# Tail rows of ten heads' query weights loaded by two DMAs of eight rows each

## The chip, the cores and the metric

One core of a Trainium2 chip runs the whole program. The metric is the device time of one execution in microseconds, the median of several runs. Inputs and outputs lie in the chip's main memory (HBM); the core works on data in SBUF, a memory of 128 partitions, and 16 DMA engines bring the data in.

## The reference

Two layers with the same weights and caches, on two rows of 448 numbers, all in float32. A layer is attention against a given cache (16 heads of 256, 4096 cached positions per row and head), then a gated feed-forward block. The core of it:

```python
def _A_ref(x, k_cache, v_cache, wq, wo):          # B=2, Sq=1, D=448, H=16, Sk=4096, Dh=256
    q = (x @ wq).reshape(B, Sq, H, Dh).transpose(0, 2, 1, 3)
    scores = jnp.einsum("bhqd,bhkd->bhqk", q, k_cache) * (Dh ** -0.5)
    p = _softmax(scores, axis=-1)
    o = jnp.einsum("bhqk,bhkd->bhqd", p, v_cache)
    return o.transpose(0, 2, 1, 3).reshape(B, Sq, H * Dh) @ wo
def _B_ref(x, W_gate, W_up, W_down):              # 448 -> 1792 -> 448
    gate = jnp.einsum("bsd,df->bsf", x, W_gate)
    up = jnp.einsum("bsd,df->bsf", x, W_up)
    return jnp.einsum("bsf,fd->bsd", gate * (gate > 0) * up, W_down)
x = A_x
x = x + _A_ref(_layernorm(x), ...)
x = x + _B_ref(_layernorm(x), ...)
x = x + _A_ref(_layernorm(x), ...)   # the second layer
x = x + _B_ref(_layernorm(x), ...)
```

## The kernel before

The two caches are 268 MB together and are needed in both layers, so nearly all of the program's traffic is the reading of K and V. A unit of work is one head and one of the two rows of x: 32 units per layer, in the order of `first`, and in the second layer backwards (`second`). The K and the V of a unit are one block of 4096 KB each, which lands as 32 KB on each of the 128 partitions. SBUF holds an arena of 27 places of 8 KB per partition: six blocks of four places, and three single places. Heads' weights always go to a single place. At the end of the first layer 22 places are kept for the second.

The loads stand in a list, `pending`, which is put together when the program is built. `pump` takes the next entry when a place is free, and writes a DMA into the queue of SyncE (SP). All of these loads stand in SP's one queue and go out in that order. An issue waits until the last reader of the place that it overwrites is done (TensorE, as a rule), and for the transfer that last used its semaphore; eight semaphores (DMAHW0 to DMAHW7 in the rows of order below) are used in turn. `release` frees a place after its last matmul and calls `pump` again. At the beginning and end of a layer blocks are split into pieces of 1024 KB or 512 KB.

The weights of a head are one load, `w_head[name]`: 1792 numbers on each of the 128 partitions. They hold, for the 448 rows of that head's query weights, three full chunks of 128 rows (3 x 256 numbers), then the remaining 64 rows (the tail), then the two chunks of the head's output weights (2 x 448). The tail is folded: the left half of its 256 columns lies on partitions 0 to 63, the right half on partitions 64 to 127, 128 numbers each.

`query` computes the query of a head for both rows of x: for each half of the 256 columns, three matmuls over the full chunks (line 309) and one over the tail (line 312). The tail's matmul takes all 128 partitions; `xT[:, FULL + j, :]` is zero on the half that doesn't belong to column half j, since `mask` is zero there. VectorE then copies the result to `q_pad` (line 317). `score` multiplies the query with a K block (line 333), `weigh` the probabilities with a V block (line 393), `project` multiplies with the output weights. `ffn` streams the feed-forward weights in seven loads `in` and four loads `out` (line 512 and line 249).

Of the kernel before, what the change touches and what calls it, by code (L numbers as in the profile page):

```python
# [14 lines left out]
B, D, H, S, DH, F = 2, 448, 16, 4096, 256, 1792  # L15
P = 128
DC = 5
FULL, TAIL = 3, 64
NT = S // P
CT = 8  # L20
UNIT = CT * DH
NC = NT // CT
BLOCKS, SINGLES = 6, 3
KEPT = 22

G, E = 4, 4
# [39 lines left out]
def two_layers(  # L66
# [3 lines left out]
    k_cache: bass.AP,  # L70
    v_cache: bass.AP,
    w_head: bass.AP,
    w_in: bass.AP,
    w_out: bass.AP,
    out: bass.AP,
):
    nc = tc.nc
# [10 lines left out]
    arena = consts.tile([P, (BLOCKS * NC + SINGLES) * UNIT], F32, name="arena")  # L88
# [8 lines left out]
    def source(key, n):  # L97
        kind, name, c = key
        if kind in "kv":
            h, b = name  # L100
            if kind == "k":
                rows = k_cache[b, h]
            else:
                rows = v_cache[b, h].rearrange("(p t) d -> p (t d)", t=NT)
            return rows[:, c * UNIT : (c + n) * UNIT]
        if kind == "h":
            return w_head[name]
        if kind == "in":
            return w_in[c]
        return w_out[:, (14 * c + 2) // 4 * D : (14 * c + 16) // 4 * D]  # L110

    def pump():
        while pending:
            at = None
            for i, ((kind, name, c), n) in enumerate(pending[: AHEAD if pending[0][1] == 1 else 1]):
                if i and kind != "h":
                    continue
                last = at_of.get((kind, name, c - 1)) if kind in "kv" else None
                at = units.take(n, kind, last)
                if at is not None:  # L120
                    break
            if at is None:
                return
            pending.pop(i)
            src = source((kind, name, c), n)
            dst = arena[:, at * UNIT : at * UNIT + src.shape[1]]
            parts = [0, src.shape[1]]
            if kind == "v" and n == 1 and c == NC - 1 and name in (first[-1], second[-1]):
                parts[1:1] = [UNIT // 2]
            if not pending:  # L130
                parts[1:1] = [src.shape[1] - D]
            for i, j in zip(parts, parts[1:]):
                nc.sync.dma_start(dst[:, i:j], src[:, i:j])
            for k in range(n):
                at_of[kind, name, c + k] = at + k

    def get(*key):
        at = at_of[key]
        return arena[:, at * UNIT : (at + 1) * UNIT]

    def release(*key):
        units.free.add(at_of.pop(key))
        pump()
# [31 lines left out]

    keep = {of_second[0], *[key for key in of_second if key[0] != "h"][:KEPT]}
    of_second = [key for key in of_second if key not in keep]
# [40 lines left out]
    xT = xr[:, :, :, 0]  # L218
# [48 lines left out]
    def again():  # L267

        for half in range(2):
            n = D - DH if half else DH  # L270
            nc.tensor.matmul(
                y[32 * half : 32 * half + B, :n], halves[:, half], yrow[:, :n],
                start=True, stop=False,
            )
# [16 lines left out]
    def attention(order, after):  # L291
# [8 lines left out]
        def query(u):  # L300
            h = order[u][0]
            w = get("h", h, 0)
            pq = pq_all
            for j in range(2):
                if j and u == 0:
                    again()
                for c in range(FULL):
                    at = c * DH + j * P
                    nc.tensor.matmul(  # L309
                        pq[:, j, :], w[:, at : at + P], xT[:, c, :], start=(c == 0), stop=False  # L310
                    )
                nc.tensor.matmul(  # L312
                    pq[:, j, :], w[:, FULL * DH : FULL * DH + P], xT[:, FULL + j, :],
                    start=False, stop=True,
                )
            q = q_pad[:, u // 2 % 2]
            nc.vector.tensor_copy(q[..., 1], pq)
            for v in (u, u + 1):
                q_of[v] = q[:, :, order[v][1]]
# [23 lines left out]
        def score_turn(u):  # L343
            s_of[u] = ps_s.tile([P, NT], F32, name="small")
            s = s_of[u].rearrange("p (h e g) -> p h e g", h=2, e=E)
            for e in range(E):
                nc.tensor.matmul(  # L347
                    s[:, :, e, :], found_s[:, e * P : (e + 1) * P], pick,
                    start=True, stop=True,
                )  # L350
# [7 lines left out]
        def softmax_exp(u):  # L358
            b = order[u][1]
            nm = work.tile([P, 1], F32, name="nm")  # L360
            nc.scalar.activation(nm, mx_of.pop(u), AF.Copy, scale=nsr[:, b : b + 1])  # L361
            p_of[u] = work.tile([P, NT], F32, name="probs")
            rs = work.tile([P, 1], F32, name="rs")
# [64 lines left out]
        def project(u):  # L428
            h = order[u][0]
            if u % 2 == 0:  # L430
                return
            wo = get("h", h, 0)[:, FULL * DH + P :]
            for c in range(2):
                add(
                    c, oT_of[h][:, c, :], wo[:, c * D : (c + 1) * D],
                    start=(c == 1 and u == 1), stop=(u == n_u - 1),
                )
            if ("h", h, 0) not in after:
                release("h", h, 0)
            if u == n_u - 1:  # L440
                busy(1, 0)
# [54 lines left out]
        busy(1, 0)  # L496
        out_keep(u)
        project(u)

    def ffn(last):  # L500
# [104 lines left out]
def _arrays(np, A_x, A_k_cache, A_v_cache, A_wq, A_wo, B_W_gate, B_W_up, B_W_down, **_):  # L605

    rows = FULL * P
    wq = A_wq.reshape(D, H, DH)
    head = [wq[c * P : (c + 1) * P].transpose(1, 0, 2) for c in range(FULL)]
    head.append(wq[rows:].reshape(TAIL, H, 2, P).transpose(1, 2, 0, 3).reshape(H, P, P))  # L610
    wo = A_wo.reshape(H, 2, P, D)
    head += [wo[:, 0], wo[:, 1]]
    full = [w[c * P : (c + 1) * P] for w in (B_W_gate, B_W_up) for c in range(FULL)]
    full.insert(FULL, np.concatenate([B_W_gate[rows:], B_W_up[rows:]]))
    down = B_W_down.reshape(4, D, D)
    chunks = [down[j, m * P : (m + 1) * P] for j in range(4) for m in range(FULL)]
    chunks += [np.concatenate([down[j, rows:], down[j + 1, rows:]]) for j in (0, 2)]
    k = A_k_cache.reshape(B, H, P, 2, E, G, 2, P).transpose(0, 1, 7, 3, 6, 5, 4, 2)
    found = {
        "x": A_x,  # L620
        "k_cache": k.reshape(B, H, P, S * 2),
        "v_cache": A_v_cache,
        "w_head": np.concatenate(head, axis=2),
        "w_in": np.stack(full),
        "w_out": np.concatenate(chunks, axis=1),
    }
    return {n: np.ascontiguousarray(a) for n, a in found.items()}
# [24 lines left out]
```

## Time and profile before

| | |
|---|---|
| time, median of 3 runs | 1325.39 us (1325.19 to 1327.15) |
| the profiled execution | 1327.24 us, of which the span is 1325.1 us |
| TensorE matmul busy | 938.0 us, 71% of the span |
| VectorE, ScalarE, GpSimd busy | 135.2, 92.1 and 47.7 us |
| DMA traffic | 561.53 MB in the main queue, 99.3% of 16 engines' time |

The span is the time from the first to the last instruction of the core that the profiler recorded; the rest of the execution lies outside it. The DMA share is the mean busy share of the 16 DMA engines: at 0.50, eight of them are busy, or all of them half the time. "The chain that ended last" follows the program back from its end, from each piece of work to what released it.

### The profile page before, as it was taken

The numbers are of one execution on the slowest core, as the hardware profiler recorded it, in microseconds if no ns is written. First come the engines' busy times: TensorE is split into PE (matmuls) and PEld (weight loads), VectorE is DVE, ScalarE is ACT, GpSimd is POOL, SyncE is SP. The second block draws the span as 40 slices with busy tenths as digits, with TensorE's granted clock in tenths as the row PEclk, the third lists the DMA queues.
The fourth block names the chain that finished last, engine by engine and source line by source line (L and its number), as shares of the span: only waits on it lengthen the run. The fifth ranks groups of instructions, "written<-read, shape, count | busy, mean of one in ns | idle before, by whom it ended". The sixth has DMA issues, their size and how long they took to land.

```text
span 1325.1 us, 13766 instructions
## 1 busy us (share of the span) xinstructions
PE 938.0 (71%) x6066; PEld 308.3 (23%) x6066; DVE 135.2 (10%) x457; ACT 92.1 (7%) x280; POOL 47.7 (4%) x134
## 2 busy tenths in 40 slices
PE   4867667767776776567688867766676676766668
PEld 2322122222221221222233322222122221222213
DVE  1101010011000110001101111010010100101100
ACT  1000000000000000000011100000000000000001
POOL 0000000000000000000000000000000000000000
PEclk9777787687667776877898897777777778778779
DMA  9999999999999999999999999999999999999997
GB/s 404 429 432 428 433 427 433 429 432 427 430 431 433 427 434 426 433 432 429 420 379 395 438 426 433 428 432 429 432 429 431 430 430 430 427 435 427 435 420 323
DMA packets 28151, 562.40 MB, mean 424 GB/s; under 512 B 3126, under 2 KB 3260, under 8 KB 10556
## 3 DMA queue, kind: packets, MB, share of 16 engines
q1 hardware_dynamic: 28084, 561.53, 99.3%
q8 instruction: 47, 0.77, 0.2%
q14 instruction: 12, 0.10, 0.0%
q10 hardware_dynamic: 8, 0.01, 0.0%
HBM read 561.52 MB, written 0.00 MB: 424 GB/s over the span
## 4 chain that ended last, share of the span: by engine, by line
PE 59%; another core or an unknown queue 21%; DMA 11%; DVE 3%; issue 1%; ACT 1%; POOL 0%; SPq 0%; POOLq 0%; ACTq 0%
PE rawa L333 12%; PE poa L393 12%; PE rawb L333 11%; PE pob L393 11%; DMA arena<-in_v_cache_dram 7%; PE small L347 4%; PE small L417 3%; PE pq L309 3%; DVE found_s L341 3%; DMA arena<-in_w_in_dram 2%; DMA arena<-in_w_out_dram 2%; PE pq L312 1%; PE y L249 1%; ACT probs L364 1%
## 5 line engine op out<-in xcount | busy, mean ns | idle before, releaser
L333 PE MATMUL rawa<-arena,q_pad 128*2 128x512 f32 x1024 | 186.0, 863 | 113.3 <-DMA arena<-in_k_cache_dram 112.8
L333 PE MATMUL rawb<-arena,q_pad 128*2 128x512 f32 x1024 | 177.4, 829 | 100.1 <-DMA arena<-in_k_cache_dram 100.1
L393 PE MATMUL poa<-arena,probs 128*2 128x512 f32 x1024 | 168.9, 821 | 62.3 <-DMA arena<-in_v_cache_dram 33.9
L393 PE MATMUL pob<-arena,probs 128*2 128x512 f32 x960 | 163.1, 841 | 47.4 <-DMA arena<-in_v_cache_dram 46.9
L347 PE MATMUL small<-ident,found_s 128*128 128x8 f32 x512 | 68.6, 260 | 35.6 <-DVE found_s L341 35.2
L347 PEld LDWEIGHTS small<-ident,found_s 128*128 128x128 f32 x512 | 62.8, 193 | 96.5 <-DVE found_s L341 96.5
L333 PEld LDWEIGHTS rawa<-arena,q_pad 128*2 128x2 f32 x1024 | 25.0, 96 | 210.9 <-issue 209.7
L393 PEld LDWEIGHTS poa<-arena,probs 128*2 128x2 f32 x1024 | 31.5, 105 | 171.6 <-issue 117.3
L361 ACT ACTIVATE nm<-top,nsr 128x1 f32<-128x1 f32 x64 | 18.8, 294 | 740.7 <-POOL top L356 740.7
L333 PEld LDWEIGHTS rawb<-arena,q_pad 128*2 128x2 f32 x1024 | 24.1, 96 | 198.3 <-DMA arena<-in_k_cache_dram 124.5
L356 POOL PARTITION_ALL_REDUCE top<-mx x64 | 22.5, 351 | 1166.1 <-DVE mx L354 1148.8
L417 PEld LDWEIGHTS small<-ones,row 128*128 128x128 f32 x256 | 43.3, 240 | 90.4 <-issue 83.9
L393 PEld LDWEIGHTS pob<-arena,probs 128*2 128x2 f32 x960 | 27.8, 105 | 156.9 <-issue 156.5
L309 PE MATMUL pq<-xs,arena 128*128 128x2 f32 x384 | 56.4, 263 | 0.0
L309 PEld LDWEIGHTS pq<-xs,arena 128*128 128x128 f32 x384 | 52.7, 208 | 2.6 <-issue 1.3
L426 DVE COPY oT<-small 128x2 f32<-128x2 f32 x64 | 10.2, 160 | 382.2 <-PE small L417 382.2
L417 PE MATMUL small<-ones,row 128*128 128x1 f32 x256 | 48.7, 294 | 0.4 <-ACT row L404 0.4
L409 DVE SCALAR_TENSOR_TENSOR row<-pob,ri,row 128x256 f32<-128x256 f32 x30 | 14.5, 484 | 205.3 <-ACT row L404 205.3
L409 DVE SCALAR_TENSOR_TENSOR row<-poa,ri,row 128x256 f32<-128x256 f32 x32 | 15.5, 484 | 170.4 <-ACT row L404 170.4
L404 ACT ACTIVATE row<-pob,ri 128x256 f32<-128x256 f32 x32 | 15.2, 474 | 231.9 <-PE pob L393 223.6
L341 DVE COPY found_s<-rawb 128x512 f32<-128x512 f32 x32 | 22.1, 692 | 88.0 <-PE rawb L333 88.0
L341 DVE COPY found_s<-rawa 128x512 f32<-128x512 f32 x32 | 22.1, 692 | 74.1 <-PE rawa L333 74.1
(81 smaller groups left out, 307.9 us busy)
## 6 DMA issues: line engine op xcount, KB each, us to landing
arena<-in_k_cache_dram SPq DMA_DIRECT2D x59, 4096.0 KB, 54.5
arena<-in_v_cache_dram SPq DMA_DIRECT2D x58, 4096.0 KB, 55.2
arena<-in_w_head_dram SPq DMA_DIRECT2D x31, 896.0 KB, 54.9
arena<-in_w_in_dram SPq DMA_DIRECT2D x14, 896.0 KB, 16.4
arena<-in_v_cache_dram SPq DMA_DIRECT2D x12, 1024.0 KB, 12.3
arena<-in_k_cache_dram SPq DMA_DIRECT2D x8, 1024.0 KB, 13.8
arena<-in_w_out_dram SPq DMA_DIRECT2D x4, 896.0 KB, 16.8
arena<-in_v_cache_dram SPq DMA_DIRECT2D x4, 512.0 KB, 47.5
```

The lines of the kernel that those rows point to most:

```text
L249: nc.tensor.matmul(bank[at : at + B, : w_h.shape[1]], stat, w_h, **flags)
L309: nc.tensor.matmul(pq[:, j, :], w[:, at : at + P], xT[:, c, :], start=(c == 0), stop=False)
L312: nc.tensor.matmul(pq[:, j, :], w[:, FULL * DH : FULL * DH + P], xT[:, FULL + j, :], start=False, stop=True,)
L333: nc.tensor.matmul(raw[u % 2][32 * g : 32 * g + 2, :], q_of[u][:, j, 1 - half : 3 - half], kt[:, g, :], start=(c == 0), stop=(c == NC - 1),)
L341: nc.vector.tensor_copy(found_s, raw[u % 2])
L347: nc.tensor.matmul(s[:, :, e, :], found_s[:, e * P : (e + 1) * P], pick, start=True, stop=True,)
L356: nc.gpsimd.partition_all_reduce(mx_of[u], mx, P, RED.max)
L361: nc.scalar.activation(nm, mx_of.pop(u), AF.Copy, scale=nsr[:, b : b + 1])
L393: nc.tensor.matmul(po_of[u][32 * t : 32 * t + 2, :], p_of[u][:, n : n + 2], vt[:, 2 * t * DH : (2 * t + 2) * DH], start=(c == 0), stop=(c ...
L404: nc.scalar.activation(row[:, :DH], po_of[u][:, :DH], AF.Copy, scale=r_of[u][:, 0:1])
L409: nc.vector.scalar_tensor_tensor(row[:, :DH], po_of.pop(u)[:, DH:], r_of[u][:, 1:2], row[:, :DH], op0=ALU.mult, op1=ALU.add,)
L417: nc.tensor.matmul(pT_of[u][:, c : c + 1], row[:, c * P : (c + 1) * P], ones, start=True, stop=True,)
```

## The change

For heads 2 to 11 the 64 tail rows leave the head's one load. The load is then 1664 numbers per partition. The tail comes as two further DMAs in front of it, each of 8 rows of 4 KB; a row holds four weight rows of 256 numbers, which go to four neighbouring partitions. The first DMA fills partitions 0 to 31, the second partitions 32 to 63. In HBM the rows are 4352 bytes apart (64 unused numbers follow each), so that a row doesn't continue the one before. The other six heads keep the folded form, whose tail now stands at the end of their load. The bytes read per head are the same.

```diff
+APART = range(2, 12)
+HEAD = FULL * DH + 2 * D
...
         if kind == "h":
-            return w_head[name]
+            return w_head[name, :, : HEAD if name in APART else HEAD + P]
...
             dst = arena[:, at * UNIT : at * UNIT + src.shape[1]]
+            if kind == "h" and name in APART:
+                for i in range(2):
+                    nc.sync.dma_start(
+                        arena[32 * i : 32 * i + 32, at * UNIT + HEAD : at * UNIT + HEAD + DH],
+                        w_tail[name, i, :, : 4 * DH].rearrange("e (r n) -> e r n", n=DH),
+                    )
...
-                nc.tensor.matmul(
-                    pq[:, j, :], w[:, FULL * DH : FULL * DH + P], xT[:, FULL + j, :],
-                    start=False, stop=True,
-                )
+                if h in APART:
+                    at = HEAD + j * P
+                    nc.tensor.matmul(
+                        pq[:, j, :], w[:TAIL, at : at + P], xT[:TAIL, FULL, :],
+                        start=False, stop=True,
+                    )
+                else:
+                    nc.tensor.matmul(
+                        pq[:, j, :], w[:, HEAD : HEAD + P], xT[:, FULL + j, :],
+                        start=False, stop=True,
+                    )
...
-            wo = get("h", h, 0)[:, FULL * DH + P :]
+            wo = get("h", h, 0)[:, FULL * DH : HEAD]
...
-    head.append(wq[rows:].reshape(TAIL, H, 2, P).transpose(1, 2, 0, 3).reshape(H, P, P))
+    tail = np.zeros((H, 2, 8, 4 * DH + 64), A_wq.dtype)
+    tail[..., : 4 * DH] = wq[rows:].transpose(1, 0, 2).reshape(H, 2, 8, 4 * DH)
     wo = A_wo.reshape(H, 2, P, D)
     head += [wo[:, 0], wo[:, 1]]
+    head.append(wq[rows:].reshape(TAIL, H, 2, P).transpose(1, 2, 0, 3).reshape(H, P, P))
```

SP's queue early in the first layer, before: one head's load, the four blocks that follow, and the next head's load. Sizes are partitions x numbers; in brackets stands what an issue waits for.

```order
L133 DMA arena<-in_w_head_dram 128x1792 [waits PE_49]
L133 DMA arena<-in_v_cache_dram 128x8192 [waits DMAHW0_49,PE_49]
L133 DMA arena<-in_k_cache_dram 128x8192 [waits DMAHW1_49,PE_49]
L133 DMA arena<-in_v_cache_dram 128x8192 [waits DMAHW3_49,DMAHW2_49,PE_49]
L133 DMA arena<-in_k_cache_dram 128x8192 [waits DMAHW4_49,PE_49]
L133 DMA arena<-in_w_head_dram 128x1792 [waits PE_49]
```

The same place in the program after: the block in front of a head, the head's three transfers, and the four blocks behind.

```order
L142 DMA arena<-in_k_cache_dram 128x8192 [waits DMAHW0_49,PE_49]
L132 DMA arena<-in_w_tail_dram 32x1x256 [waits DMAHW1_49]
L132 DMA arena<-in_w_tail_dram 32x1x256 [waits DMAHW2_49]
L142 DMA arena<-in_w_head_dram 128x1664 [waits DMAHW3_49,PE_49]
L142 DMA arena<-in_v_cache_dram 128x8192 [waits DMAHW4_49,PE_49]
L142 DMA arena<-in_k_cache_dram 128x8192 [waits DMAHW5_49,PE_49]
L142 DMA arena<-in_v_cache_dram 128x8192 [waits DMAHW6_49,PE_49]
L142 DMA arena<-in_k_cache_dram 128x8192 [waits DMAHW7_49,PE_49]
```

Two tail transfers now stand ahead of a head's load, so there are seven issues instead of five for every four blocks, and the turn of the eight semaphores comes round sooner.

TensorE, the query of one head in the first layer, before, with the first V product behind it:

```order
L309 MATMUL pq<-xs,arena 128x2 [waits DMAHW2_49]
L309 MATMUL pq<-xs,arena 128x2 x2
L312 MATMUL pq<-xs,arena 128x2
L309 MATMUL pq<-xs,arena 128x2 x3
L312 MATMUL pq<-xs,arena 128x2
L393 MATMUL pob<-arena,probs 2x512 [waits DMAHW3_49,Activation_49]
```

The same after:

```order
L318 MATMUL pq<-xs,arena 128x2 [waits DMAHW4_49]
L318 MATMUL pq<-xs,arena 128x2 x2
L323 MATMUL pq<-xs,arena 128x2 [waits DMAHW3_49,DMAHW2_49]
L318 MATMUL pq<-xs,arena 128x2 x3
L323 MATMUL pq<-xs,arena 128x2
L409 MATMUL pob<-arena,probs 2x512 [waits DMAHW5_49,Activation_49]
```

The number and order of the matmuls are the same; the tail's matmul (line 323 after) now waits for the two tail transfers.

## Rows read from the trace of the kernel before

**Rows 1.** The page: span; queues with packets, MB, share of 16 engines.
```profile
span 1325.1 us, 13766 instructions
...
q1 hardware_dynamic: 28084, 561.53, 99.3%
q8 instruction: 47, 0.77, 0.2%
```

**Rows 2.** Windows: engines, granted clock, DMA share, GB/s, 300 to 600 us.
```profile
300.00:600.00 300.00, 210.53 (x1282) 65.11 (x1276) 28.59 (x93) 17.79 (x57) 10.27 (x28) 0.73 1.00 430
```

**Rows 3.** The chain that ended last, 100 to 145 us.
```profile
108.90 5.31 PE poa L393 x32
114.21 4.27 another core or an unknown queue
118.52 3.59 PE rawb L333 x16
```

**Rows 4.** Short windows at the end, columns as in rows 2.
```profile
1316.75:1317.00 0.25, 0.25 (x12) 0.21 (x5) 0.00 (x0) 0.00 (x0) 0.00 (x0) 1.00 0.57 237
...
1317.25:1317.50 0.25, 0.25 (x9) 0.10 (x7) 0.00 (x0) 0.00 (x0) 0.00 (x0) 1.00 0.48 201
...
1319.00:1320.00 1.00, 0.94 (x17) 0.45 (x16) 0.00 (x0) 0.00 (x0) 0.00 (x0) 1.00 0.41 160
...
1320.25:1320.50 0.25, 0.21 (x4) 0.09 (x4) 0.00 (x0) 0.09 (x1) 0.00 (x0) 1.00 0.06 22
1320.50:1320.75 0.25, 0.25 (x5) 0.20 (x3) 0.00 (x0) 0.25 (x1) 0.00 (x0) 1.00 0.00 0
```

**Rows 5.** Short windows between the layers, columns as in rows 2.
```profile
666.00:667.00 1.00, 1.00 (x12) 0.71 (x14) 0.16 (x1) 0.00 (x0) 0.00 (x0) 1.00 1.02 423
670.00:670.25 0.25, 0.25 (x8) 0.06 (x4) 0.00 (x0) 0.00 (x0) 0.00 (x0) 1.00 0.62 258
...
670.50:670.75 0.25, 0.25 (x8) 0.00 (x0) 0.00 (x0) 0.00 (x0) 0.00 (x0) 1.00 0.48 201
...
672.25:672.50 0.25, 0.00 (x0) 0.00 (x0) 0.00 (x0) 0.00 (x0) 0.00 (x0) 1.00 0.69 258
672.50:672.75 0.25, 0.00 (x0) 0.00 (x0) 0.00 (x0) 0.00 (x0) 0.00 (x0) 1.00 1.04 401
```

**Rows 6.** The chain: start, us, what; between layers and at the end.
```profile
654.71 16.45 DMA arena<-in_w_in_dram
...
672.45 8.51 DMA arena<-in_w_in_dram
...
1302.39 16.83 DMA arena<-in_w_out_dram
...
1322.47 0.38 ACT found_s L596
```

**Rows 7.** Issues, first layer: KB each, median us to landing.
```profile
arena<-in_k_cache_dram SPq DMA_DIRECT2D x27, 4096.0 KB, 55.2
arena<-in_w_head_dram SPq DMA_DIRECT2D x13, 896.0 KB, 56.1
```

**Rows 8.** Issues of the last weights: KB each, us to landing.
```profile
arena<-in_w_out_dram SPq DMA_DIRECT2D x1, 448.0 KB, 15.7
arena<-in_w_out_dram SPq DMA_DIRECT2D x1, 224.0 KB, 14.1
```

**Rows 9.** Line 312: its matmul in ns, who waits for it.
```profile
L312 PE MATMUL pq<-xs,arena x128: 251/251/354, 21.4 to 1254.7; 128*128 128x2 f32 x128
  DVE q_pad L317: 60.8, 32
```

**Rows 10.** Waits of SP's queue: us in total, times, longest.
```profile
SPq L133 <- DMA arena<-in_k_cache_dram: 226.0, 57, 10.8
```

**Rows 11.** SP's issues in order of time, 105 to 115 us.
```profile
105.16 0.33 SPq L133 DMA_DIRECT2D arena<-in_k_cache_dram  x1
...
114.27 0.33 SPq L133 DMA_DIRECT2D arena<-in_v_cache_dram  x1
```

More of the change, by code (lines that the diff above doesn't have):

```diff
@@ L72, in two_layers @@
     w_head: bass.AP,
+    w_tail: bass.AP,
     w_in: bass.AP,
@@ L623, in _arrays @@
         "w_head": np.concatenate(head, axis=2),
+        "w_tail": tail,
         "w_in": np.stack(full),
```

## The prediction

> **What bounds the kernel now.** I read the page first, then windows of the middle of a layer, then the chain, then short windows where the stream of data stops. The page gives a span of 1325.1 us in which the main queue's packets take 99.3% of the time of 16 DMA engines [rows 1]. From 300 to 600 us the DMA share is 1.00 at 430 GB/s while TensorE is busy for 210.53 of 300 us [rows 2]. In the chain, TensorE ends its products with a V block at 114.21 us and then waits 4.27 us for the next K block [rows 3]; only one core runs, so the "unknown queue" there is a transfer. One DMA engine moves 430 / 16 = 26.9 GB/s; a block of 4096 KB takes 9.75 us. So the 16 engines' time is the bound, and a transfer has landed only when the last of its engines is done.
>
> That matters at two places, where the chain waits for a transfer and the stream runs out. At the end the chain waits 16.83 us, until 1319.2, for output weights, and its last work starts at 1322.47 [rows 6]. In the short windows there the DMA share doesn't fall from 1 to 0 at once: it is 0.57 before 1317.0, 0.48 after 1317.25 (7.7 engines), 0.41 on the mean of 1319 to 1320, 0.06 in the quarter before 1320.50, and then 0 [rows 4]. Eight engines are done by 1317.0 and eight work on to 1320.4. I call them the early and the late half; the early half's slowest has **3.4 us** of room. Between the layers the chain waits for gate weights until 671.2 and again until 681.0 [rows 6]; the share falls from 1.02 to 0.62 at 670.0 and 0.48 at 670.5, and new transfers fill it at 672.50 [rows 5]. There the early half's slowest is done near 670.7 and the late half goes on to at least 672.5: room of **1.8 us** or more, since the refill hides the late half's end.
>
> Why two halves? The instruction queue moved 47 packets, 0.77 MB, 0.2% of 16 engines' time [rows 1]: 0.002 x 16 x 1325 = 42 us. Over eight engines that is 5 us each, the size of the lag seen; so I take it that instruction fetches burden eight of the engines. No row names an engine.
>
> **The change, part by part.** *Bytes.* Both versions move 64 KB of tail rows per head, and each head is loaded once in each layer, so ten heads give ten loads per layer, all well inside it. Before, every engine carried 4 KB of them: 4096 / 26.9 = 152 ns. After, that is gone from every engine's share of the head's load, and two transfers of 32 pieces of 1 KB come in. If each is dealt out by the source's eight rows, eight engines get four pieces of each, eight pieces per head.
>
> *Price of a piece.* At the full rate eight are 8192 / 26.9 = 305 ns. Small pieces cost more: from 1319 to 1320 the rate is 160 / (0.41 x 16) = 24.4 GB/s per busy engine [rows 4], and what is still to come then are 448 and 224 KB transfers [rows 8], 3.5 and 1.75 KB per partition. Against 26.9 that is 6.8 ns lost on a piece of 1.75 KB and 13.7 on one of 3.5 KB. A piece of 1 KB so takes 45 to 52 ns, eight take 359 to 415. I take 359, the nearer row by size. Gaps between transfers: the share reads 1.00 over 300 us, so under 1.5 us is lost in it, to some 36 transfers (65 such issues in 540 us; the two shapes shown are 40 of them [rows 7]): at most 0.04 us each, 0.8 us for a layer's 20 new ones.
>
> *So, per layer:* engines without pieces 10 x 152 = **1.5 us less**; engines with them 10 x (359 - 152) = **2.1 us more**, from 1.5 (full rate) to 2.6 (415), and 3.4 with every gap.
>
> *Who gets the pieces.* No row here shows where a transfer of eight rows goes. I take eight engines, because the source hands out eight rows and its padding keeps them apart, and the early half as a judgement that rows can't support; the two other ways are priced below. [...]
>
> *End of layer 2.* The late half ends 1.5 us sooner, the early half's slowest at -3.4 + 2.1 = -1.3. The later counts: **-1.3 us** (-1.5 at full rate, -0.8 at 415 ns, 0 with every gap).
>
> *Between the layers.* Late half -1.5; early half -1.8 + 2.1 = +0.3 (-0.3, +0.8, +1.6). As the room may be more than 1.8, I take **0**. If the first attention's last blocks and the gate weights don't land sooner, nothing in the second layer starts sooner.
>
> *SP.* Forty more issues of 0.33 us [rows 11] are 13 us, in a queue that waits 226.0 us for K blocks alone [rows 10]: hidden. If that cover were gone they would cost at most those 13 us. What is queued behind them matters more. SP uses eight semaphores in turn, and an issue waits for the transfer eight places before. With seven transfers to four blocks instead of five, that is no longer always an old one: in the order after, the first tail waits for the K block of eight rows before, with four newer blocks queued between; the V block behind it waits for the head before those four. So at least 4 x 9.75 = 39 us of work is queued when SP goes on. Today a block lands 55.2 us after its issue, 5.7 blocks [rows 7]; I expect some 49. The engines don't run dry: nothing.
>
> *TensorE.* The last matmul of a query takes 64 rows instead of 128: still one matmul of 251 ns for each half [rows 9]. It waits for two semaphores more, of transfers issued ahead of the head itself. Only the copy of the query waits for it, and the chain spends 4.27 us per block on data [rows 3]: nothing; without that cover, tens of ns per query.
>
> **Sum.** 0 - 1.3 = -1.3 us. The profiled execution took 1327.24 us (span 1325.1 and 2.1 around it), so 1325.9; it lies 1.85 above the median, and on the median, 1325.39, it is **1324.1 us**.
>
> **The rivals.** *Both ends gain* the late half's 1.5 us: if the late half really ends past 672.5 (room of 3.6 instead of 1.8 is enough), then -3.0, **1322.4**. For it: the hidden end; against it: the share already drops to 0.48 at 670.5.
>
> *The change doesn't do what it says*: the pieces go to all 16 engines, four each per head: 4 x 45 - 152 = +28 ns, 0.3 us per layer, **1326.0**. The source's padded rows speak against it. [...]
>
> *The early half overshoots*: with every gap, +1.6 between the layers and 0 at the end, -0.1 taken as nothing: **1327.0**. It begins to cost where pieces add more than 1.8 us per layer. For it: small transfers on half the engines; against it: a share of 1.00 across many transfer borders.
>
> *The pieces fall on the late half*: it is 2.1 us later at both ends, +4.2, **1329.6**, slower. No row excludes it; it is paid in full as soon as the eight engines are those that also fetch instructions.
>
> *The queue runs dry* behind the new semaphore waits: 0.2 us lost at each of 20 loads would be +4, 1329 or so. It needs the 39 us to be gone, which rows 7 speak against.
>
> **How the numbers follow.** Main case 0.47, both ends gain 0.20, all 16 engines 0.10, overshoot 0.10, late half 0.08, dry queue 0.05. A difference under 0.2%, 2.65 us, is about what a measurement of this kernel can't tell from none: the lines are 1322.7 and 1328.0. Faster: 0.20 and a sliver of the main case, 0.21. Slower: 0.08 + 0.05 = 0.13. Same: 0.66. The main case's own bounds (-0.3 and -1.5; +0.8 and -0.8) are 1323.6 to 1325.4. The range goes down to 1322.2 for both ends, and up to 1326.8, past the 16-engine case and most of the overshoot; outside are 0.13 and some of the overshoot.
>
> **What would show it.** After: the share at the end falls from 1 to 0 within about 1.5 us, with no plateau near 0.5; the last data lands about 1.3 us sooner; between the layers the plateau shrinks too, but the refill stays at 672.5; head loads read 832 KB and 40 transfers of 32 KB appear; K blocks land some 49 us after their issue. A longer plateau would mean that the late half got the pieces; an unchanged one, all 16. The prediction is wrong if the first layer's end moves by more than a microsecond.

## The result, and the profile after

The change takes 1328.38 us (median of 11 runs, 1327.81 to 1330.66) against 1325.62 of the kernel before (11 runs on the same chip, 1324.22 to 1327.67): ratio 1.0021, 95% interval 1.0013 to 1.0029. It is slower by about 2.8 us, where 1324.1 was predicted. The profiled execution took 1328.03 us, 0.4 below its median; that of before, 1327.24, lies 1.6 above its own. So this pair of traces differs by only 0.8 us in time, and has to be compared place by place.

The page of the change, as in [rows 1], and the window from 300 to 600 us, as in [rows 2]:

```profile
span 1326.2 us, 13847 instructions
...
q1 hardware_dynamic: 29684, 561.53, 99.2%
q8 instruction: 48, 0.79, 0.2%
```

```profile
300.00:600.00 300.00, 218.13 (x1272) 70.78 (x1268) 28.29 (x93) 17.80 (x57) 10.32 (x28) 0.71 1.00 430
```

The bytes are the same, the stream in the middle of a layer runs at 430 GB/s with a share of 1.00 as before, and there are 1600 packets more: 40 transfers with 32 pieces and eight finishing packets each. The instruction queue moved 48 packets where it moved 47.

Short windows at the end (engines' busy time, granted clock, DMA share, GB/s), which answer to [rows 4]:

```profile
1316.75:1317.00 0.25, 0.25 (x6) 0.23 (x6) 0.00 (x0) 0.00 (x0) 0.00 (x0) 1.00 0.65 258
...
1317.25:1317.50 0.25, 0.25 (x3) 0.01 (x3) 0.19 (x1) 0.00 (x0) 0.00 (x0) 1.00 0.60 237
...
1319.00:1320.00 1.00, 1.00 (x10) 0.34 (x4) 0.00 (x0) 0.00 (x0) 0.00 (x0) 1.00 0.12 50
...
1320.25:1320.50 0.25, 0.23 (x5) 0.11 (x8) 0.00 (x0) 0.00 (x0) 0.00 (x0) 1.00 0.14 57
1320.50:1320.75 0.25, 0.25 (x10) 0.23 (x6) 0.00 (x0) 0.00 (x0) 0.00 (x0) 1.00 0.09 36
...
1321.00:1321.25 0.25, 0.25 (x7) 0.00 (x0) 0.00 (x0) 0.00 (x0) 0.00 (x0) 1.00 0.11 43
...
1321.50:1321.75 0.25, 0.25 (x4) 0.16 (x6) 0.00 (x0) 0.25 (x1) 0.00 (x0) 1.00 0.00 0
```

Before, the share stood near one half and fell to 0 at 1320.5. Now it falls to 0.12 from 1319 to 1320 and stays at 0.09 to 0.14 until 1321.25. A share of 0.125 is two of 16 engines, so I read it as two engines that work on alone for over two microseconds. The last data comes 1.0 us later. The same between the layers, as in [rows 5]:

```profile
670.00:670.25 0.25, 0.07 (x2) 0.04 (x1) 0.00 (x0) 0.16 (x2) 0.00 (x0) 1.00 0.75 315
...
670.50:670.75 0.25, 0.25 (x4) 0.25 (x4) 0.00 (x0) 0.00 (x0) 0.00 (x0) 1.00 0.70 287
...
672.50:672.75 0.25, 0.25 (x8) 0.00 (x0) 0.00 (x0) 0.00 (x0) 0.00 (x0) 1.00 0.14 57
...
674.00:674.25 0.25, 0.25 (x4) 0.00 (x0) 0.00 (x0) 0.00 (x0) 0.00 (x0) 1.00 0.20 86
...
674.50:674.75 0.25, 0.00 (x0) 0.00 (x0) 0.00 (x0) 0.00 (x0) 0.00 (x0) 1.00 1.05 430
```

At 672.50, where before new transfers filled the stream, the share is now 0.14, and at 674.00 it is 0.20; the refill comes at 674.5, 2.0 us later. The chain, as in [rows 6]:

```profile
656.83 16.42 DMA arena<-in_w_in_dram
...
674.32 7.66 DMA arena<-in_w_in_dram
...
1305.68 15.71 DMA arena<-in_w_out_dram
...
1323.56 0.38 ACT found_s L612
```

The first wait for gate weights ends at 673.25 (before 671.16), 2.1 us later; the second at 681.98 (before 680.96), 1.0 later. The second wait itself took 8.51 us in the profiled execution of before and 7.66 here. In ten of the eleven traces of other kernels below it is 7.6 to 7.7, and in one (sixteen engines) 8.84, so the 0.85 us seem to belong to that execution of before and not to the kernel. The last work starts 1.09 us later.

All these times stand on one clock. So the 1.09 us at the end are the whole loss of this pair, and no second loss on top of the 2.1: from the end of the second wait to the last work 641.5 us pass before and 641.6 after. What the pair shows is a loss of 2.1 us between the layers. How much the second layer adds to make up the 2.8 us of the medians it can't tell, since its execution of before is itself 1.6 us slower than the median.

What the other steps rested on: issues from 60 to 600 us, as in [rows 7] (the page gives no landing times here), SP's waits as in [rows 10], two of its issues as in [rows 11], and the tail's matmul as in [rows 9].

```profile
arena<-in_w_head_dram SPq DMA_DIRECT2D x9, 832.0 KB
...
arena<-in_w_tail_dram SPq DMA_DIRECT2D x18, 32.0 KB
```

```profile
SPq L142 <- DMA arena<-in_v_cache_dram: 462.5, 63, 10.6
SPq L142 <- DMA arena<-in_k_cache_dram: 295.6, 40, 10.8
SPq L132 <- DMA arena<-in_k_cache_dram: 168.0, 18, 9.4
```

```profile
118.68 1.44 SPq L132 DMA_DIRECT2D arena<-in_w_tail_dram  x2
120.22 0.38 SPq L142 DMA_DIRECT2D arena<-in_w_head_dram  x1
```

```profile
L323 PE MATMUL pq<-xs,arena x80: 247/268/371, 87.3 to 1172.2; 64*128 64x2 f32 x80
```

Two tail issues took 1.44 us together, some 0.7 each and not 0.33; forty are 28 us. SP waits 168.0 us for K blocks at just these issues, so they are still hidden. The tail's matmul takes 268 ns (median) where it took 251.

### The profile page after: what moved, and what is told of

The parts are those of the page before. It is cut to its first block, busy times and chain, and to the rows that moved or that the text cites. A ratio compares the mean times of both kernels' runs of the same rounds, so it can differ in the third digit from the quotient of the medians.

```text
span 1326.2 us, 13847 instructions
## 1 busy us (share of the span) xinstructions
PE 966.5 (73%) x6066; PEld 324.1 (24%) x6066; DVE 133.5 (10%) x457; ACT 92.1 (7%) x280; POOL 47.9 (4%) x134
## 4 chain that ended last, share of the span: by engine, by line
PE 58%; another core or an unknown queue 23%; DMA 12%; DVE 3%; issue 2%; ACT 1%; POOL 1%; SPq 0%; POOLq 0%; ACTq 0%; DVEq 0%
PE rawa L349 12%; PE pob L409 11%; PE poa L409 11%; PE rawb L349 10%; PE small L363 5%; DMA arena<-in_k_cache_dram 4%; PE pq L318 3%; DMA arena<-in_v_cache_dram 3%; DMA arena<-in_w_in_dram 3%; PE small L433 3%; DVE found_s L357 2%; DMA arena<-in_w_out_dram 2%; PE pq L323 1%; PE y L258 1%
## 5 line engine op out<-in xcount | busy, mean ns | idle before, releaser
L349 PE MATMUL rawa<-arena,q_pad 128*2 128x512 f32 x1024 | 183.2, 850 | 93.0 <-DMA arena<-in_k_cache_dram 92.4
L409 PE MATMUL poa<-arena,probs 128*2 128x512 f32 x1024 | 173.1, 839 | 74.0 <-DMA arena<-in_v_cache_dram 42.7
L409 PE MATMUL pob<-arena,probs 128*2 128x512 f32 x960 | 173.8, 890 | 48.2 <-DMA arena<-in_v_cache_dram 48.2
L363 PE MATMUL small<-ident,found_s 128*128 128x8 f32 x512 | 73.7, 271 | 33.6 <-DVE found_s L357 33.3
L363 PEld LDWEIGHTS small<-ident,found_s 128*128 128x128 f32 x512 | 67.9, 206 | 93.9 <-DVE found_s L357 93.9
L318 PE MATMUL pq<-xs,arena 128*128 128x2 f32 x384 | 61.1, 275 | 0.0
L318 PEld LDWEIGHTS pq<-xs,arena 128*128 128x128 f32 x384 | 57.0, 222 | 2.9 <-issue 1.3
L433 PE MATMUL small<-ones,row 128*128 128x1 f32 x256 | 49.8, 298 | 0.4 <-ACT row L420 0.4
```

Source lines behind the costliest of these rows:

```text
L318: nc.tensor.matmul(pq[:, j, :], w[:, at : at + P], xT[:, c, :], start=(c == 0), stop=False)
L349: nc.tensor.matmul(raw[u % 2][32 * g : 32 * g + 2, :], q_of[u][:, j, 1 - half : 3 - half], kt[:, g, :], start=(c == 0), stop=(c == NC - 1),)
L363: nc.tensor.matmul(s[:, :, e, :], found_s[:, e * P : (e + 1) * P], pick, start=True, stop=True,)
L409: nc.tensor.matmul(po_of[u][32 * t : 32 * t + 2, :], p_of[u][:, n : n + 2], vt[:, 2 * t * DH : (2 * t + 2) * DH], start=(c == 0), stop=(c ...
L433: nc.tensor.matmul(pT_of[u][:, c : c + 1], row[:, c * P : (c + 1) * P], ones, start=True, stop=True,)
```

## Which engine does what, worked out from the packets

The trace gives start, length, size and queue of each packet, but not its engine. From 300 to 600 us of the trace of before, 5147 of the main queue's 5217 packets start 3 or 4 ns before the end of another. I take that other to be the packet ahead on the same engine, and assume that every engine takes its share of each transfer in the queue's order; so each packet can be put to one of 16 sequences. This is such a reconstruction, not a view of the profile. "Fetch" are the 16 KB packets of the instruction queue, some 1.06 us each, which come mostly every 20 to 40 us, in the reconstruction in turn on eight engines; the few 8 KB packets of a second instruction queue are not counted. The numbers say how many us before the last engine the others were done with the load of gate weights that the chain waits for first between the layers. In the trace of the change the last two landings on that load's semaphore are at 673.18 and 673.26 us, and the wait ends with the last.

```
                     pieces + fetch   pieces only   fetch only    neither
before               -                -             0 to 2.0 (8)  1.7 to 5.2 (8)
the change           0, 0.1 (2)       1.5 to 4.4    3.6 to 5.6    8.2, 8.6
six source rows      0 (1)            1.6 to 4.0    3.8 to 5.6    8.3 to 8.6
four source rows     none             0 to 2.1      1.9 to 4.0    5.9 to 7.0
```

Before, the engines that fetch are last, six of them clear of all others, as the prediction took it. The change puts its pieces on eight engines, but these are neither the early nor the late half: **six of them don't fetch, two do**. These two end 1.5 us or more behind all others. The last two rows are experiments below. In the second layer of the change the two are last again, and all others are 1.8 us or more ahead of them.

Mean length of a packet of the main queue in ns, by its size in bytes, and their count; 6656 is a shortened head load's, 7168 that of a whole one and of the gate weights, 32768 that of a block:

```
                    1024 (512)     6656           7168           32768
before              -              -              280.7 x6272    1218.8 x14976
the change          46.1 x1282     258.4 x2560    279.7 x3712    1218.8 x14976
16 engines          47.1 x1282     285.9 x2560    284.8 x3712    1222.9 x14976
without padding     47.9 x1282     286.1 x2560    280.0 x3712    1222.4 x14976
six engines, 5 part. 48.1 x642     279.8 x1280    279.7 x4992    1220.6 x14976
upper partitions    49.8 x1282     300.5 x2560    280.3 x3712    1224.5 x14976
folded apart        27.5 x2560*    261.0 x2560    280.0 x3712    1218.7 x14976
```

The star marks packets of 512 B.

## The experiments

Theory at first: two of the eight engines fetch, and they set both ends. Rivals: small transfers cost something on all engines; a threshold or the semaphores' turn. Each expectation names its theories by letters of its own group of runs. That the fetched instructions are TensorE's, as some of them have it, is the author's assumption, which no trace shows. All times are medians, beside runs of the kernel before on the same chip: 1325.37 us in the first group of four, 1325.59 in the second group of four, 1326.14 in the last three.

**Sixteen engines.** Each transfer has 16 source rows of two partitions.

```diff
-                        w_tail[name, i, :, : 4 * DH].rearrange("e (r n) -> e r n", n=DH),
+                        w_tail[name, i, :, : 2 * DH].rearrange("e (r n) -> e r n", n=DH),
...
-    tail = np.zeros((H, 2, 8, 4 * DH + 64), A_wq.dtype)
+    tail = np.zeros((H, 2, 16, 2 * DH + 64), A_wq.dtype)
...
```

> The same ten heads, the same two transfers in front of each head's load, the same places in SP's queue and the same matmuls, but each transfer has 16 rows of two partitions instead of 8 rows of four. Theory A (the pieces load eight engines, and two of these also fetch TensorE's instructions, so these two finish last at both ends): with 16 rows every engine gets 4 pieces of 46 ns per head and loses 152 ns, +0.03 us per head, +0.6 us in all: 1326.2 against 1325.6, and a plateau of half the engines at the end as in the kernel before. Theory B (the two transfers themselves cost: three issues for one, semaphores that come round sooner, a queue less deep): as slow as the change, 1328.4. Theory C (all small pieces are dearer than 46 ns): at least as slow as the change.

Measured: 1334.89 us, ratio 1.0074 (1.0061 to 1.0087): far slower than theories A and B had it. Theory C has the sign (at least as slow as the change) but not the cause. The packet table shows where the time goes: the pieces are cheap (47.1 ns), but the packets of the heads' loads behind them take 285.9 instead of 258.4 ns, and blocks 4.1 ns more each. 2560 x 27.5 + 14976 x 4.1 + 3712 x 5.1, over 16 engines, is 9.4 us, near the whole loss of 9.5. Something else than the number of bytes per engine is at work.

**Six engines, five heads.** Two transfers of six rows of five partitions and one of four single rows, for heads 2, 4, 6, 8 and 10.

```diff
-APART = range(2, 12)
+APART = range(2, 12, 2)
...
-                for i in range(2):
+                for p, e, r in ((0, 6, 5), (30, 6, 5), (60, 4, 1)):
...
```

> Five heads (2, 4, 6, 8, 10); the tail comes as three transfers: two of 6 rows of five partitions and one of 4 rows of one partition, so that the pieces should load six engines instead of eight (10 or 11 pieces each, +0.31 to +0.36 us per head; all others -0.15). Theory A, if the two engines that also fetch are the last two of the eight: these now save 0.15 us per head; between the layers the other engines use up their room of 1.8 (5 x 0.36), no gain; at the end -0.8 us: 1324.8 to 1325.4, and no plateau of two engines. If the two are among the first six: +1.6 per layer, 1328.8. Theory B: eight issues for four blocks at five heads instead of seven at ten: slower than before by about half of what the change costs, 1327.

Measured: 1331.67, ratio 1.0051 (1.0039 to 1.0064). It was meant to take the pieces off two engines, but here too the head's packets grew, to 279.8 ns. It tells nothing about the two engines.

**Five heads.** The change itself, for heads 2, 4, 6, 8 and 10 alone.

```diff
-APART = range(2, 12)
+APART = range(2, 12, 2)
```

> The change at five heads (2, 4, 6, 8, 10) instead of ten, nothing else. Theory A: the two engines were level with the last ones before, so they are last from the first head on, and the loss goes with the number of heads: 5 x 0.21 = 1.0 us per layer, 1327.0 to 1327.6 (half of the change's 2.8), with two engines left at the end for about half as long. A threshold (room used up first, as the prediction had it) would show 1325.0 or less here. Theory B: half of the change's loss as well, 1327.

Measured: 1327.13 (11 runs), ratio 1.0012 (1.0003 to 1.0021): 1.8 us for five heads, 2.8 for ten. Five heads already lose, where an overshoot past a room was to show 1325.0 or less. That the loss grows with the heads fits, but the intervals overlap (0.4 to 2.8 us and 1.7 to 3.8). A cost of the transfers as such forecast the same time, and this run doesn't tell it apart. The head's packets are short here, 258.0 ns.

**Six engines, other heads in each layer.** As "six engines", for heads 2, 5 and 8 in the first layer and 2 to 9 in the second.

```diff
-APART = range(2, 12)
+APART = ((2, 5, 8), range(2, 10))
...
```

> Six engines as in the run with three transfers, but three heads in the first layer (2, 5, 8), where the engines that don't fetch have 1.8 us of room, and eight in the second (2 to 9), where they have 3.4. Theory A: the fetching engines save 0.5 us in the first layer and 1.2 in the second, the six use 1.1 of 1.8 and 2.9 of 3.4: -0.5 and -0.5 to -1.2, 1324.0 to 1324.6 against 1325.6. Theory B: slower than before, above 1326.5.

Measured: 1332.97, ratio 1.0061 (1.0048 to 1.0073), with the same long packets of the heads (280.1 ns). It shares the defect of the run with six engines and says nothing on the two layers.

What the slow kernels had in common was how a source row's pieces were laid on the partitions: in groups of two or five, where the change has four. The next group moves the groups of four to other partitions, and tries fewer engines with the groups as they are.

**Upper partitions.** The same transfers onto partitions 64 to 95 and 96 to 127. If the number of engines or of transfers made those kernels slow, this one takes the change's 1328.4 us; if the partitions did, it takes longer.

```diff
-                        arena[32 * i : 32 * i + 32, at * UNIT + HEAD : at * UNIT + HEAD + DH],
+                        arena[TAIL + 32 * i : TAIL + 32 * i + 32, at * UNIT + HEAD : at * UNIT + HEAD + DH],
...
-                        pq[:, j, :], w[:TAIL, at : at + P], xT[:TAIL, FULL, :],
+                        pq[:, j, :], w[TAIL:, at : at + P], xT[TAIL:, FULL + 1, :],
```

> The change with the same two transfers of 8 rows of four partitions, but onto partitions 64 to 95 and 96 to 127 instead of 0 to 31 and 32 to 63; the matmul reads the weights and x there. [...]

Measured: 1341.37, ratio 1.0118 (1.0104 to 1.0132): 13 us over the change for the same pieces and the same number of finishing packets (320 more than before in both). The head's packets take 300.5 ns; 2560 x 42.1 + 14976 x 5.7 over 16 engines is 12.1 us. The destination is all that differs (and with it the partitions that the tail's matmul reads), so the destination decides. In the window of [rows 2] the stream moves 426 GB/s for 430, still with a share of 1.00: engines are busy, but slower.

```profile
300.00:600.00 300.00, 209.59 (x1264) 67.06 (x1253) 28.13 (x92) 17.80 (x57) 10.27 (x28) 0.73 1.00 426
```

**Without padding.** The change, with the source rows one behind the other.

```diff
-    tail = np.zeros((H, 2, 8, 4 * DH + 64), A_wq.dtype)
+    tail = np.zeros((H, 2, 8, 4 * DH), A_wq.dtype)
```

> The change without the 64 unused numbers behind each source row, so that the 8 rows follow one another in memory. If the padding decides how the transfer is dealt out, it now goes to 16 engines with two partitions each, as in the run with 16 rows: 1334.9. If the 8 rows are kept apart anyway: as the change, 1328.4.

Measured: 1335.9, ratio 1.008 (1.0067 to 1.0093), as the run with 16 engines. There are 640 finishing packets more than before, 16 for each of 40 transfers: the rows no longer keep the transfer on eight engines. The padding in the change does what the prediction took it to do, and without it the change would have cost 10 us.

**Folded apart.** The tail keeps its folded form on 128 partitions, but as one transfer of its own with 512 B per partition.

```diff
-                for i in range(2):
-                    nc.sync.dma_start(
-                        arena[32 * i : 32 * i + 32, at * UNIT + HEAD : at * UNIT + HEAD + DH],
-                        w_tail[name, i, :, : 4 * DH].rearrange("e (r n) -> e r n", n=DH),
-                    )
+                nc.sync.dma_start(
+                    arena[:, at * UNIT + HEAD : at * UNIT + HEAD + P], w_tail[name]
+                )
...
```

> [...] Theory B (separate transfers and semaphores that come round sooner cost by themselves; six issues for four blocks instead of five): about half of the change's loss or more, 1327 to 1328.

Measured: 1327.58 (11 runs), ratio 1.0017 (1.0006 to 1.0028), 2.0 us slower. Spread evenly over 16 engines, the 2560 pieces and 320 finishing packets of 20 transfers are eight pieces of 27.5 ns and a finishing packet of 9 for each engine and head, for the 170 ns that eight packets of the head's load get shorter (279.7 - 258.4 = 21.3 each). That is 59 ns a head, 1.2 us for 20 loads, inside the interval (0.8 to 3.7 us) though below its middle. The time itself lies in the range of theory B, the cost of separate transfers, and 0.8 us above what the even load gives. So this run doesn't rule out B. The run with two source rows below bounds it: its forty transfers and their pieces cost 1.0 us over the run without a tail. Small pieces cost time here, 2.0 us, even when by this count no engine gets more than another.

**Six source rows.** The change with six of the eight rows in each transfer. 16 of the 64 tail rows of ten heads are left out, and only the first 24 are used.

```diff
-                        arena[32 * i : 32 * i + 32, at * UNIT + HEAD : at * UNIT + HEAD + DH],
-                        w_tail[name, i, :, : 4 * DH].rearrange("e (r n) -> e r n", n=DH),
+                        arena[32 * i : 32 * i + 24, at * UNIT + HEAD : at * UNIT + HEAD + DH],
+                        w_tail[name, i, :6, : 4 * DH].rearrange("e (r n) -> e r n", n=DH),
...
```

> The change with 6 rows in each of the two transfers instead of 8, so that 16 of the 64 tail rows of the ten heads are neither loaded nor used: the pieces of the seventh and eighth of the engines are taken away, and nothing else. Theory A (the loss is that of two engines that carry pieces and fetch TensorE's instructions, and they are these two): every fetching engine now saves 1.5 us per layer, the six others use up the room between the layers (+0.3) and keep a little at the end (-1.3): 1324.3 to 1325.0, and no plateau of two engines. Theory D (the pieces cost by being there, whoever moves them): three quarters of the change's loss, 1327.4.

Measured: 1329.24 (8 runs), ratio 1.0027 (1.0017 to 1.0038): no gain, where the theory had one of some 4 us. It assumed that the two engines that fetch are the last two of the eight. Windows of its end (columns as above):

```profile
1318.00:1319.00 1.00, 1.00 (x16) 0.68 (x19) 0.19 (x1) 0.00 (x0) 0.00 (x0) 1.00 0.65 258
1319.00:1320.00 1.00, 1.00 (x24) 0.53 (x15) 0.00 (x0) 0.00 (x0) 0.00 (x0) 1.00 0.21 84
1320.00:1321.00 1.00, 1.00 (x13) 0.42 (x7) 0.00 (x0) 0.00 (x0) 0.00 (x0) 1.00 0.12 47
1321.00:1322.00 1.00, 1.00 (x17) 0.45 (x17) 0.00 (x0) 0.00 (x0) 0.00 (x0) 1.00 0.06 25
1322.00:1323.00 1.00, 0.94 (x16) 0.31 (x7) 0.00 (x0) 0.38 (x1) 0.00 (x0) 1.00 0.04 14
```

From 1321 on the share is 0.06 and 0.04, as if one engine of 16 (0.0625) worked alone, until past 1322. The reconstruction agrees: one of the two is still among the six. So it fits the theory that an engine with both duties sets the ends, and not the guess where the two engines are. What was missing was a run in which neither gets pieces. Three runs follow: two with the same forty transfers, pieces per engine and semaphores, one without them.

**Four source rows.** As above with four rows (partitions 0 to 15 and 32 to 47); 32 of 64 tail rows are left out, and 16 are used.

```diff
-                        arena[32 * i : 32 * i + 32, at * UNIT + HEAD : at * UNIT + HEAD + DH],
-                        w_tail[name, i, :, : 4 * DH].rearrange("e (r n) -> e r n", n=DH),
+                        arena[32 * i : 32 * i + 16, at * UNIT + HEAD : at * UNIT + HEAD + DH],
+                        w_tail[name, i, :4, : 4 * DH].rearrange("e (r n) -> e r n", n=DH),
...
```

> Left out: of the 64 tail rows of ten heads only 32 are loaded (4 source rows of four partitions in each of the two transfers), and 16 of these are used. Everything else is that of the change. Theory F: as with two source rows, 1323 to 1325 if none of the four engines fetches for TensorE, 1328 to 1329.5 if one does; the run with the fetching engine among its pieces shows one engine working on alone, the run without shows none. Theory D: 1328 to 1329 in both. The six-row run (1329.24) had one fetching engine left among its six; so with fewer engines the time must fall by some 4 us at the step at which that engine drops out, and not gradually.

Measured: 1324.75 (11 runs), ratio 0.9987 (0.9978 to 0.9996).

```profile
1314.00:1315.00 1.00, 1.00 (x15) 0.45 (x13) 0.00 (x0) 0.00 (x0) 0.00 (x0) 1.00 0.76 308
1315.00:1316.00 1.00, 0.95 (x9) 0.20 (x10) 0.00 (x0) 0.00 (x0) 0.00 (x0) 1.00 0.55 215
1316.00:1317.00 1.00, 1.00 (x16) 0.41 (x16) 0.00 (x0) 0.00 (x0) 0.00 (x0) 1.00 0.13 52
1317.00:1318.00 1.00, 0.94 (x9) 0.40 (x8) 0.00 (x0) 0.38 (x1) 0.00 (x0) 1.00 0.09 18
```

The share is still 0.55 from 1315 to 1316 and the data is there before 1318, where in the change two engines go on alone until past 1321:

```profile
1320.00:1321.00 1.00, 0.98 (x18) 0.45 (x16) 0.00 (x0) 0.00 (x0) 0.00 (x0) 1.00 0.13 50
1321.00:1322.00 1.00, 0.94 (x14) 0.40 (x8) 0.00 (x0) 0.38 (x1) 0.00 (x0) 1.00 0.10 31
```

In the reconstruction none of the four engines fetches.

**Two source rows.** As above with two rows; 48 of 64 tail rows are left out, and 8 are used.

```diff
-                        arena[32 * i : 32 * i + 32, at * UNIT + HEAD : at * UNIT + HEAD + DH],
-                        w_tail[name, i, :, : 4 * DH].rearrange("e (r n) -> e r n", n=DH),
+                        arena[32 * i : 32 * i + 8, at * UNIT + HEAD : at * UNIT + HEAD + DH],
+                        w_tail[name, i, :2, : 4 * DH].rearrange("e (r n) -> e r n", n=DH),
...
```

> Left out: of the 64 tail rows of ten heads only 16 are loaded (2 source rows of four partitions in each of the two transfers), and eight of these are used. The number of transfers, their place and the semaphores are those of the change; each engine that gets pieces gets as many as in the change. Theory F: if neither of the two engines fetches instructions for TensorE, the last engines are 3 us lighter and the two have room of more than 1.5 us at both ends: 1323 to 1325. If one of them does, it works on alone at both ends as in the change: 1328 to 1329.5, and the share at the end stands at 0.1 for 2 us or more. Theory D (forty more transfers with their semaphores cost the 2.8 us): 1328 to 1329, whichever engines they are.

Measured: 1323.93 (11 runs), ratio 0.9983 (0.9974 to 0.9992). In the reconstruction the two engines don't fetch, and at the end of the second layer they are 0.6 and 2.1 us ahead of the last engine, which does. At the end of the first layer one of them is the last, by 1.1 us, so the expected room of 1.5 us at both ends isn't quite there; the time is within the expected range.

**No tail.** The ten heads' tail rows are left out altogether; the shortened head loads stay.

```diff
-            if kind == "h" and name in APART:
-                for i in range(2):
-                    nc.sync.dma_start(
-                        arena[32 * i : 32 * i + 32, at * UNIT + HEAD : at * UNIT + HEAD + DH],
-                        w_tail[name, i, :, : 4 * DH].rearrange("e (r n) -> e r n", n=DH),
-                    )
...
```

> Left out: the 64 tail rows of ten heads (heads 2 to 11) are neither loaded nor used; their head loads stay at 1664 numbers per partition. Theory F (the last of the 16 engines sets the time; the change gives work to engines that also fetch instructions): every engine has 20 times 152 ns less to do, 3.0 us, so about 1322.6 us against 1325.6 before, faster by 1.6 to 3.5 us. Theory D (the loss of the change comes with the split of the head's load, its different size and place, not with engines): the loads of 1664 numbers alone already cost, and the time is 1325 to 1328.

Measured: 1322.91 (7 runs), ratio 0.9973 (0.9963 to 0.9984), 3.2 us faster; 20 x 170 ns are 3.4.

```profile
1315.00:1316.00 1.00, 1.00 (x10) 0.34 (x4) 0.00 (x0) 0.00 (x0) 0.00 (x0) 1.00 0.52 197
1316.00:1317.00 1.00, 0.93 (x16) 0.45 (x16) 0.00 (x0) 0.00 (x0) 0.00 (x0) 1.00 0.30 118
1317.00:1318.00 1.00, 1.00 (x17) 0.39 (x8) 0.00 (x0) 0.38 (x1) 0.00 (x0) 1.00 0.06 23
```

Here the share is 0.52 until 1316, the plateau of half the engines that [rows 4] show of before, only sooner. So with 0, 2, 4, 6 and 8 source rows the time against before is -3.2, -2.2, -1.4, +3.7 and +2.8 us. (Six and eight rows don't differ beyond their intervals.) The step of 5 us lies between four and six, where by the reconstruction the first engine with both duties comes in. The transfers don't grow there: two, four, six and eight rows have the same forty. The bytes grow evenly, and with them the partitions that are filled. A cost of transfers and semaphores as such of the size of the loss would have shown with two rows already, which are only 1.0 us over none, and the splitting of the head's load would have with none.

No kernel here that does all the work beats the one before. The four-row kernel leaves out half the tail of ten heads, 76 ns a load on every engine by the 152 of the prediction; brought back evenly over 20 loads that is 1.5 us, all of its gain.

## Why the prediction was wrong

*What bounds the kernel* was right: leaving out 170 ns per load on every engine gave 3.2 us, nearly one for one, and the last engine sets both ends.

*Eight engines get the pieces*: right. There are 320 finishing packets more for 40 transfers (3442 of 4 bytes for 3122), eight each. I read their number as that of the engines: each of the 195 loads of before has 16 (3122, with two of the output). With 2, 4, 6 and 8 rows of four partitions there are 80, 160, 240 and 320 more for 40 transfers, one for each row; with 16 rows of two, and with eight that follow one another in memory, 640. Which engines these are no run shows; that smaller sets lie within larger ones fits what was seen.

*Price of a piece*: right, 46.1 ns for 45 taken, and in the reconstruction with no gap between transfers. 8 x 46.1 and two finishing packets of 9 ns are 387 ns; less the 170 that the head's load loses, 217 a head, 2.2 us a layer where the prediction had 2.1. The bytes taken off were worth 170 ns, not 152, as measured packets show.

*Who gets the pieces* is **the step that failed**. The prediction put all eight on the early half, "as a judgement that rows can't support", and priced the late half as a rival at 0.08 (1329.6). By the reconstruction and the plateau of two, the engines with pieces are neither: six that don't fetch and two that do. Two are enough, since the last engine counts and not the half. The rival was nearest, and its sentence that 4.2 us are paid as soon as the eight engines are those that also fetch needed one word less: as soon as one of them does. Between the layers that price is paid in full: 2.1 us, by the 2.2 worked out above. The reconstruction has the two among the six that were last before: of the six that only fetch in the change, four end 3.6 to 3.9 us ahead and two 5.5 and 5.6, much the same gap as between the six and the other two before. Why the whole is 2.8 and not 4.2 us stays open, since this pair of traces has the second layer no longer than before.

*Why two halves*: the halves were there, but the working for them was short by half. The 5 us per engine are for the whole run, and the engines start level again between the layers (the share is back at 1.04 after 672.50 [rows 5]), so 2.6 us fall to a layer, where lags up to 5 were seen. In the reconstruction a fetch costs its engine more than its own 1.06 us: the 32 KB packet behind it takes 1.7 us for 1.2, so some 1.5 us in all, about three times a layer.

*Between the layers*: predicted 0, and at most a microsecond; the first wait there ends 2.1 us later. *End of layer 2*: predicted -1.3; the last data lands 1.0 us later, both layers together. Both signs follow from the failed step. What the prediction named as the sign, a longer plateau if the late half got the pieces, came in another form: not eight engines for longer, but two.

*SP and its semaphores*: right in what it is worth, nothing. The issue's price was off (0.70 for 0.33 us), and hidden. The page gives no landing times for the change's blocks; worked out from the packets, as above, K blocks from 60 to 600 us land a median of 50.5 us after their issue (before, by the same working, 54.0 for the page's 55.2), near the 49 expected. The share of 1.00 over 300 us and the run with two rows show that the queue doesn't run dry. *TensorE*: 17 ns more per tail matmul, hidden.

*The rival of all 16 engines* was priced at 1326.0. Run, it took 1334.89: the price of the pieces was right (47.1 ns for 45), and a cost was missing that no row of before shows: with rows of two partitions the packets of the heads' loads take 285.9 instead of 258.4 ns.

## What to carry to other kernels

Where 16 DMA engines share a stream and the program waits for the last, look for who is last and why before giving some of them extra work: a plateau in the share at the end suggests how many are late (0.5 is eight, 0.125 two), though not whether the extra work meets the same ones. Half an assignment was enough to lose here: by the reconstruction, one engine with both burdens set the time (1329.24 us with one such engine among six, 1324.75 with none among four). A cheap test is to cut the number of engines that get the work, with all else kept, and look for a step.

## What the runs showed of the hardware

The same 1 KB pieces of eight engines cost 13 us more per 40 transfers of 32 KB when they go to partitions 64 to 127 instead of 0 to 63 (1341.37 against 1328.38). The pieces themselves grow little (49.8 for 46.1 ns), but the 6656-byte packets around them take 300.5 instead of 258.4 ns on the mean and even blocks 5.7 ns more. Rows of two partitions (285.9 ns), rows of five (279.8 and 280.1) and the rows without padding (286.1) lengthen them too, on partitions 0 to 63. With the change's rows of four there, and with 512 B on each of 128 partitions, they take 258.4 and 261.0. Why the layout on the partitions costs this no run shows.

Instruction fetches take 0.2% of the DMA engines' time here, and yet they decide which engine ends last. In the reconstruction 47 packets of some 1.06 us, dealt out in turn to eight engines, each costing its engine some 1.5 us with the packet behind it, put those up to 5 us behind the others by the end of a layer.
